# The second feed-forward of an attention, expert and feed-forward kernel: from one pass over its inner dimension to two

## The chip, the cores and the metric

The kernel runs on one core of one Trainium2 chip. The core has a matrix engine (PE, with PEld for the loading of its stationary operands), a vector engine (DVE), an activation engine (ACT), a general engine (POOL) and a queue engine that only issues transfers (SP). ACT and POOL can issue transfers too, each from its own row of instructions. The metric is the device time of one execution in microseconds (us), lower is better; the time to beat is the median of three runs.

## The reference, cut to what matters

```python
def reference(**kwargs):
    attn_out = _attn_ref(q, k, v)          # local + downsampled attention, 4 x 8 heads, 576 tokens, 64 each
    x = attn_out.transpose(0, 2, 1, 3).reshape(2304, 512)
    x = _moe_ref(x, w_gate, w1, w2)        # 8 experts, 288 tokens each
    return _moe2_ref(x, w_in, w_out)       # the second feed-forward

def _moe_ref(x, w_gate, w1, w2):
    ...                                    # greedy: the largest logits first, at most 288 tokens per expert
    for e in range(E):
        mask = assigned == e
        h = np.maximum(x[mask] @ w1[e], 0.0)      # 512 -> 1024
        out[mask] = h @ w2[e]                     # 1024 -> 512

def _moe2_ref(x, w_in, w_out):
    h = x @ w_in                                  # 512 -> 2048
    sp = np.where(h > 20.0, h, np.log1p(np.exp(np.minimum(h, 20.0))))
    g = h * np.tanh(sp)
    return (g @ w_out).astype(np.float32)         # 2048 -> 512
```

The host hands `w_in` and `w_out` over as 64-bit floats.

## The kernel before

**The number format.** Matrix products are made to near float32 precision out of a faster format: each operand is split into a high part (a cast, L623 on ACT or L621 on DVE, tiles `wah`, `wbh`, `gh`) and a low part (operand minus high part, L626 on POOL or DVE, tiles `wal`, `wbl`, `gl`), and each product is three matmuls (`mm3`, L631 to L633). Only the first expert, E0, is "plain" (`N32 = 1`): it multiplies unsplit float32 (L707).

**The stages.** The front end (attention, tokens 0 to 2303) writes `x` to DRAM. Then come eight routing phases, each of which finds the 288 tokens of one expert by many small DVE and PE steps, and eight experts E0 to E7. Expert k gathers its rows of `x` (L650, transfers issued by POOL) and computes; its result, split into high and low parts, goes to a ring of 768 tokens in on-chip memory, `Yh` and `Yl`. The second feed-forward runs in groups: M4 takes four tiles of 128 tokens out of the ring, M2 two. There are five groups, four M4 and one M2 at the end, called M#0 to M#4 here. `ORDER` puts experts and groups in a row: R0, N2, R1, E0, E1, M4, E2, E3, M4, E4, E5, M4, E6, E7, M4, M2; the two numbers behind a name are how many routing steps and how many pieces of narrowing (below) are put beside each of its steps. The instructions of each engine then follow a scheduler's order, and each engine runs its own row in order.

**Narrowing.** `Narrow` turns the 64-bit words of `w_in` and `w_out` into float32, in 32 pieces of 128x512. A piece is loaded by SP (L541, tile `n`) or sits in its final place already, passes ACT (L565, L567), DVE (L570, L573, L575, L578), POOL or DVE (L581, L583), and ends with an addition on POOL (L585) that puts the float32 weights into `wM_sb`, where they stay.

**A step of a group.** An M4 group has 16 steps, one for each slice f of 128 of the 2048 inner columns; the M2 group has 8 steps of two slices. In each step the weights of the slice are split anew (`split`: `wah`/`wal` of `w_in`, `wbh`/`wbl` of `w_out`), since the parts are not kept; PE makes `hm` (12 matmuls of 512 columns, of 256 where the tokens wrap around the ring and in M#4); ACT and DVE turn it into the activation, by turns: ACT L782, DVE L783, ACT L784, L785, L786, DVE L791, L792, L794, ACT L797 (`gh`), DVE L798 (`gl`); and PE adds `g` times `w_out` into `oa` some steps later (12 matmuls of 512 columns for four tiles). After the last slice the result is doubled into `osb` (L755 ACT, L757 DVE) and POOL scatters it to the output (L758).

**The buffers.** The raw words of the expert weights, `wraw` (L711, loaded by SP in pieces of 128x1024 4-byte words), and the raw pieces `n` of narrowing share a ring of three slots (`NRW`).

Of the kernel before, what the change touches and what calls it, by code (L numbers as in the profile page):

```python
# [57 lines left out]
class Attn:  # L58
# [190 lines left out]
    def emit(self, nar=None, rload=None):  # L249
# [65 lines left out]
class Router:  # L315
# [47 lines left out]
    def phase(self, k):  # L363
# [111 lines left out]
        V.tensor_scalar_add(ig, it, 1152.0)  # L475
        ip = self.psr.tile([96, 3], F32, name="ip", tag="rt")
# [18 lines left out]
        self.out[k] = idx, exi  # L495
# [3 lines left out]
POOLN = 4  # L499
NV = 3  # L500
N32 = 1
PE4 = 2
COPY2, COPY4 = 4, 8
LASTM = 1
LIGHT, PN1, GL1, T1 = 0, 1000, 1, 0
LAG2 = 3
NMI, NRW, NWA, NWB, NGS = 4, 3, 3, 6, 4
# [11 lines left out]
class Narrow:  # L519

    def __init__(self, nc, a, ne, zp):
        self.nc, self.a, self.zp = nc, a, zp
        self.ne = ne
        self.raw = {}
        self.n = 0

    def load(self, i, n=1, eng=None):

        s = (i if i < self.ne else i - self.ne) + 1
        t = self.a['wM_t'][s >= self.ne]
        s0 = s - self.ne * (s >= self.ne)
        (eng or self.nc.sync).dma_start(t[:, s0:s0 + n].rearrange("p s n -> p (s n)").bitcast(I32), self.a['wM'].rearrange("p f n -> p (f n)")[:, 512 * i:512 * (i + n)].bitcast(I32))
        for j in range(n):
            self.raw[i + j] = t[:, s0 + j].bitcast(I32).rearrange("p (n t) -> p n t", t=2)

    def stage(self, i):
        st = self.raw[i] = self.st.tile([128, 512, 2], I32, name="n64", tag="wraw")
        f, h = divmod(i, 2)  # L540
        self.nc.sync.dma_start(st.rearrange("p n t -> p (n t)"), self.a['wM'][:, f, 512 * h:512 * h + 512].bitcast(I32))  # L541

    def slot(self, f, s):
        return self.a['wM_t'][f >= self.ne][:, f - self.ne * (f >= self.ne), s]
# [5 lines left out]
    def steps(self):  # L550
# [5 lines left out]
        f, h = divmod(i, 2)  # L556
        b = {}
        def begin():
            if i not in self.raw:
                self.stage(i)  # L560
            st = self.raw.pop(i)
            z = self.zp.tile([128, 512], F32, name="nz")
            b.update(z=z, zi=z.bitcast(I32), w=self.slot(f, slice(512 * h, 512 * h + 512)), hi=st[:, :, 1], lo=st[:, :, 0])
            b['u'] = b['w'].bitcast(I32)
            nc.scalar.activation(out=b['z'], in_=b['hi'].bitcast(F32), func=AF.Abs)  # L565
            if i % NV:
                nc.scalar.activation(out=b['lo'].bitcast(F32), in_=b['lo'].bitcast(U32), func=AF.Copy, scale=2.0 ** -52)  # L567
# [16 lines left out]
        def end():  # L584
            nc.gpsimd.tensor_tensor(out=b['w'], in0=b['w'], in1=b['z'], op=ALU.add)  # L585
        return [begin, clip, bits, sign, power, low, end]

class FFN:

    LAG = 2  # L590

    def __init__(self, nc, tc, ctx, a, ps, slot):
        self.slot = slot
        self.nc, self.tc, self.a, self.ps = nc, tc, a, ps
        P = lambda n, b: ctx.enter_context(tc.tile_pool(name=n, bufs=b))
# [18 lines left out]
    def split(self, src, pool, nm):  # L614
# [4 lines left out]
        self.ncopy += 1  # L619
        if self.ncopy % self.copyn == 0:  # L620
            nc.vector.tensor_copy(wh, src)  # L621
        else:
            nc.scalar.copy(wh, src)  # L623
# [20 lines left out]
    def gather(self, k, idx):  # L644
        nc = self.nc
        nc.sync.dma_start(self.a['ilist'][288 * k:288 * k + 288, :].rearrange("(g p) o -> p (g o)", g=3), idx)
        rows = []
        for g in range(3):
# [3 lines left out]
            rows.append(xr)  # L652
        return rows

    def expert(self, k, rows, exi):
# [20 lines left out]
        def second(j, w2, hh, hl):  # L676
# [9 lines left out]
            if j == 7:  # L686
# [3 lines left out]
                for c in range(4):  # L690
                    for s0, s1 in pieces:
# [3 lines left out]
                                                in1=self.Yh[:, c, q:q + s1 - s0].bitcast(F32), op=ALU.subtract)  # L695
        for j in range(8):
# [26 lines left out]
    def group(self, t0, nt, last=False):  # L723

        nc, ps = self.nc, self.ps
        n = 128 * nt

        ms = [512 // n] * (16 * n // 512)
        if last and n < 512:
            ms[len(ms) - LASTM:] = [1] * (512 // n * LASTM)  # L730
        q = 128 * t0 % RING
        cols = [(0, n)] if q + n <= RING else [(0, RING - q), (RING - q, n - RING + q)]
        ixs = self.ix.tile([128, 4], I32, name="ixs")
        nc.sync.dma_start(ixs[:, 0:nt], self.a['ilist'][128 * t0:128 * (t0 + nt), :].rearrange("(t p) o -> p (t o)", p=128))
# [111 lines left out]
def body(nc, tc, a):  # L846
    with ExitStack() as ctx:
# [33 lines left out]
        for st in ORDER:  # L881
# [9 lines left out]
            if st[0] == 'E':  # L891
                while k not in rows:
                    bg[0]()
# [23 lines left out]
```

## Time and profile before

| | |
|---|---|
| median of three runs | 1049.76 us (1044.21 to 1050.76) |
| the profiled execution | 1053.49 us |
| its span, first to last instruction | 1051.7 us |
| mean granted PE clock | 0.929 |
| busy share: PE, PEld | 86%, 70% |
| busy share: DVE, ACT, POOL | 74%, 52%, 43% |
| read from and written to DRAM | 75.08 MB, 9.45 MB |

All the rows below are of the profiled execution, on its own scale of time. "Busy" is the time in which an engine executes; the matmuls of PE overlap at their ends, so the time from one start to the next tells the price of one. A row `A <- B` names the tile written and the tiles read.

### The profile page before, as it was taken

What the parts mean: (1) busy time and instruction counts of PE and PEld (TensorE: products, weight loads), DVE (VectorE), ACT (ScalarE), POOL (GpSimd) and SP (SyncE); (2) the same over time, 40 slices, a digit from 0 to 9 for tenths busy, and PEclk for the clock granted to TensorE, in tenths of its full rate; (3) what the DMA queues carried; (4) which work ended last, traced back from release to release, by engine and by line L of the source; (5) the groups of instructions that cost most, each with busy time, mean ns of one, the idle gap of its engine ahead of it and who ended that gap; (6) DMA issues with size and microseconds to landing.
All of it is one profiled execution on the core that took longest, in us unless ns stands there. A gap on an engine that the chain in (4) does not pass through costs nothing. (4 is left out here: it accounts for less than half of the span.)

```text
span 1051.7 us, 18198 instructions
## 1 busy us (share of the span) xinstructions
PE 903.4 (86%) x6676; PEld 739.2 (70%) x6676; DVE 780.6 (74%) x1798; ACT 545.7 (52%) x1310; POOL 448.1 (43%) x402
## 2 busy tenths in 40 slices
PE   5999994248778787998898999999899999999986
PEld 3777773135557565777897888898776798776774
DVE  4798988938958999878458767646877653777785
ACT  3677783103224455554436556555566555666663
POOL 4443403434636755326343322535432444333562
PEclk9999995558989898999899989999999999999998
DMA  8559516262253311015520001532200350000010
GB/s 210 150 158 274 177 55 230 80 163 81 63 124 101 80 41 60 1 44 162 125 78 1 1 1 41 165 120 62 22 1 21 131 173 1 1 1 1 1 41 20
DMA packets 32905, 85.69 MB, mean 81 GB/s; under 512 B 8912, under 2 KB 9168, under 8 KB 32048
## 3 DMA queue, kind: packets, MB, share of 16 engines
q1 hardware_dynamic: 26816, 67.23, 22.3%
q0 software_dynamic: 2976, 9.44, 4.0%
q10 hardware_dynamic: 3024, 7.87, 2.1%
q8 instruction: 52, 0.85, 0.3%
q14 instruction: 37, 0.30, 0.1%
HBM read 75.08 MB, written 9.45 MB: 80 GB/s over the span
## 5 line engine op out<-in xcount | busy, mean ns | idle before, releaser
L626 POOL TENSOR_TENSOR wal<-wM_sb,wah 128x512 fp32r<-128x512 f32 x80 | 115.1, 1441 | 164.2 <-ACT wah L623 160.0
L631 PE MATMUL hm<-Yh,wah 128*128 128x512 f32 (+1 forms) x384 | 135.6, 353 | 6.1 <-DVE eu L794 3.0
L633 PE MATMUL hm<-Yh,wal 128*128 128x512 f32 (+1 forms) x384 | 134.1, 349 | 2.6 <-POOL wal L626 2.6
L632 PE MATMUL hm<-Yl,wah 128*128 128x512 f32 (+1 forms) x384 | 133.6, 348 | 1.1 <-DVE Yl L694 1.1
L631 PE MATMUL oa<-wbh,gh 128*128 128x512 f32 x288 | 119.6, 415 | 11.4 <-ACT gh L797 11.0
L626 POOL TENSOR_TENSOR wal<-wraw,wah 128x512 fp32r<-128x512 f32 x56 | 73.9, 1325 | 119.9 <-ACT wah L623 119.4
L633 PE MATMUL oa<-wbh,gl 128*128 128x512 f32 x288 | 116.9, 409 | 3.1 <-DVE gl L798 3.1
L632 PE MATMUL oa<-wbl,gh 128*128 128x512 f32 x288 | 116.2, 403 | 0.0
L797 ACT CAST gh<-eu 128x512 fp32r<-128x512 f32 (+1 forms) x73 | 44.6, 611 | 105.8 <-DVE eu L794 105.8
L791 DVE SCALAR_TENSOR_TENSOR eu<-eu,r 128x512 f32<-128x512 f32 (+1 forms) x73 | 67.3, 922 | 39.0 <-ACT r L786 39.0
L631 PEld LDWEIGHTS hm<-Yh,wah 128*128 128x128 f32 x384 | 74.9, 195 | 17.1 <-ACT wah L623 4.7
L626 POOL TENSOR_TENSOR wbl<-wM_sb,wbh 128x512 fp32r<-128x512 f32 x40 | 53.8, 1345 | 75.0 <-ACT wbh L623 74.9
L633 PEld LDWEIGHTS hm<-Yh,wal 128*128 128x128 f32 x384 | 75.1, 196 | 11.1 <-POOL wal L626 3.2
L632 PEld LDWEIGHTS hm<-Yl,wah 128*128 128x128 f32 x384 | 74.9, 195 | 10.8 <-issue 1.6
L792 DVE SCALAR_TENSOR_TENSOR eu<-eu,r 128x512 f32<-128x512 f32 (+1 forms) x73 | 80.0, 1096 | 1.3
L784 ACT ACTIVATE eu<-eu,one_sb 128x512 f32<-128x512 f32 (+1 forms) x73 | 52.2, 716 | 48.2 <-DVE eu L783 47.5
L631 PEld LDWEIGHTS oa<-wbh,gh 128*128 128x128 f32 x288 | 56.7, 197 | 28.3 <-ACT gh L797 17.9
L633 PEld LDWEIGHTS oa<-wbh,gl 128*128 128x128 f32 x288 | 56.0, 195 | 23.6 <-DVE gl L798 12.0
L623 ACT CAST wah<-wM_sb 128x512 fp32r<-128x512 f32 x80 | 48.6, 612 | 45.6 <-PE hm L632 31.7
L631 PE MATMUL hp<-xh,wah 128*128 128x288 f32 x224 | 69.0, 309 | 0.2 <-DVE eu L794 0.2
L626 DVE TENSOR_TENSOR wbl<-wraw,wbh 128x512 fp32r<-128x512 f32 x56 | 41.6, 744 | 36.6 <-ACT wbh L623 32.2
L632 PE MATMUL ya<-gl,wbh 128*128 128x288 f32 x224 | 67.6, 302 | 0.0
(177 smaller groups left out, 2499.0 us busy)
## 6 DMA issues: line engine op xcount, KB each, us to landing
wraw<-in_wE_dram SPq DMA_DIRECT2D x56, 512.0 KB
n<-in_wM_dram SPq DMA_DIRECT2D x20, 512.0 KB
vw<-in_vw_dram SPq DMA_DIRECT2D x16, 315.0 KB
kT<-in_kT_dram SPq DMA_DIRECT2D x16, 291.0 KB
qT<-in_qT_dram SPq DMA_DIRECT2D x16, 288.0 KB
vd<-in_vd_dram SPq DMA_DIRECT2D x16, 288.0 KB
x_dram<-xr ACTq DMA_DIRECT2D x18, 256.0 KB
w<-in_wE_dram SPq DMA_DIRECT2D x16, 256.0 KB
```

Of the source, the lines that this page charges most:

```text
L623: nc.scalar.copy(wh, src)
L626: eng.tensor_tensor(out=wl, in0=src, in1=wh.bitcast(F32), op=ALU.subtract)
L631: mm(out, lh, rh, start=first, stop=False)
L632: mm(out, lh, rl, start=False, stop=False)
L633: mm(out, ll, rh, start=False, stop=last)
L784: nc.scalar.activation(out=u, in_=e, func=AF.Square, bias=one)
L791: nc.vector.scalar_tensor_tensor(out=u, in0=u, scalar=1.0, in1=r, op0=ALU.add, op1=ALU.mult)
L792: nc.vector.scalar_tensor_tensor(out=u, in0=u, scalar=2.0, in1=r, op0=ALU.subtract, op1=ALU.mult)
L797: nc.scalar.copy(gh[:, 0:w], e)
```

## The change

The groups take two tiles (256 tokens) and half of the inner dimension. Nine groups G (half 0) each write their sum, doubled, to a DRAM buffer `part`; nine groups P (half 1) load it, add it, and scatter the result. A group has four steps of two slices. So that the second pass can have the tokens again, each expert also writes its split result to a DRAM buffer `y_dram` (ACT issues the stores), and each P group loads its 256 tokens of it back into the ring (POOL issues the loads).

The split parts of the feed-forward's weights are made once, at the end of each piece of narrowing, and kept: the pieces of half 0 in `wM1`, on chip; those of half 1 (pieces 16 to 31) in the slot of the raw ring in which they were loaded, from where POOL stores them to the DRAM buffer `wB`. After E7 the pools of the experts are closed and eight transfers of 1 MB (POOL) fetch half 1 into `wM3`, in their place. The groups split no weights.

Besides: E1 is plain too (`N32 = 2`); the raw ring has four slots; no piece is loaded or narrowed during the front end; routing and narrowing have other rates; the list of tokens is written in rows; `eu`, `r` and `osb` have rings of their own.

```diff
-NRAW, NNAR, NKL, NSL, NKP, NSP = 6, 0, 24, 0.5, 42, 1.4
-N32 = 1
+N32 = 2
-NMI, NRW, NWA, NWB, NGS = 4, 3, 3, 6, 4
+NRW, NWA, NWB, NGS = 4, 3, 5, 4
+HC = 8
+LAGE, LAGM = 2, 3
 class Narrow:
...
+    def fetch(self, i, n, eng):
+        f = i // 2
+        t, f0 = self.a['wM_t'][-1]
+        eng.dma_start(t[:, f - f0:f - f0 + n // 2].rearrange("p f h n -> p (f h n)"), self.a['wB'][:, 1024 * (i - 2 * HC):1024 * (i - 2 * HC + n)])
...
         def begin():
-            if i not in self.raw:
-                self.stage(i)
-            st = self.raw.pop(i)
+            rt = self.st.tile([128, 1024], I32, name="n64", tag="wraw")
+            nc.sync.dma_start(rt, self.a['wM'].rearrange("p f n -> p (f n)")[:, 512 * i:512 * i + 512].bitcast(I32))
+            raw = rt.rearrange("p (n t) -> p n t", t=2)
+            st = self.place(i) if i < 2 * HC else rt.bitcast(F32R)
...
         def end():
-            nc.gpsimd.tensor_tensor(out=b['w'], in0=b['w'], in1=b['z'], op=ALU.add)
+            nc.gpsimd.tensor_tensor(out=b['t'], in0=b['t'], in1=b['z'], op=ALU.add)
+            h, l = b['st'][:, 0:512], b['st'][:, 512:1024]
+            nc.scalar.copy(h, b['t'])
+            nc.gpsimd.tensor_tensor(out=l, in0=b['t'], in1=h.bitcast(F32), op=ALU.subtract)
+            if i >= 2 * HC:
+                nc.gpsimd.dma_start(self.a['wB'][:, 1024 * (i - 2 * HC):1024 * (i - 2 * HC + 1)].bitcast(F32), b['st'].bitcast(F32))
...
+                for s0, s1 in pieces:
+                    q = (pos + s0) % RING
+                    for v, y in enumerate((self.Yh, self.Yl)):
+                        nc.scalar.dma_start(self.a['y_dram'][:, v, :, 288 * k + s0:288 * k + s1].bitcast(F32), y[:, :, q:q + s1 - s0].bitcast(F32))
...
-    def group(self, t0, nt, last=False):
+    def group(self, t0, half):
...
+        nt, n, m = 2, 256, 2
+        ms = [m] * (HC // m)
...
+        if half:
+            for v, t in enumerate((self.Yh, self.Yl)):
+                nc.gpsimd.dma_start(t[:, :, y], self.a['y_dram'][:, v, :, 128 * t0:128 * t0 + n])
...
+            for t in range(nt):
+                os[t] = self.mi.tile([128, 512], F32, name="osb")
+                nc.sync.dma_start(os[t], self.a['part'][128 * (t0 + t):128 * (t0 + t) + 128, :])
...
+                    if not half:
+                        o = self.mi.tile([128, 512], F32, name="osb")
                         nc.scalar.activation(out=o, in_=acc[t], func=AF.Copy, scale=2.0)
+                        nc.scalar.dma_start(self.a['part'][128 * (t0 + t):128 * (t0 + t) + 128, :], o)
+                        continue
+                    o = os[t]
+                    nc.vector.scalar_tensor_tensor(out=o, in0=acc[t], scalar=2.0, in1=o, op0=ALU.mult, op1=ALU.add)
...
             for i in range(m):
-                w1 = self.split(self.slot(f + i, slice(0, 512)), self.wa, "wa")
-                w2.append(self.split(self.slot(f + i, slice(512, 1024)), self.wb, "wb"))
...
+                w1 = self.slot(HC * half + f + i, 0)
...
-ORDER = 'R0 N2 R1 E0/0.6/2 E1/0.8/0.5 M4/1/1 E2/0.6/2 E3/0.8/0 M4/0.5/0 E4/0.3/0 E5/0/0 M4/0.9/0 E6/1.2/0 E7/0.3/0 M4/0.6/0 M2/0/0'.split()
+ORDER = ('R0 R1 E0/0/1 R2 E1/0/1 G/1 E2/0.8/0.3 G/0.8 E3/0.85/0.3 G/0.8 E4/0.85/0.3 G/0.8 E5/0.85/0.3 G/0.8 E6/0.85/0.3 G/0.8 E7/0/0.6 N'
+         + ' G' * 3 + ' P' * 9).split()
...
             if st[0] == 'N':
-                advance(1, k)
+                while nar.n < 32:
+                    nar.piece()
+                f.flush()
+                ctx_e.close()
+                wM.append((P("wM3", ctx).tile([128, 16 - HC, 2, 1024], F32R, name="wM3_sb"), HC))
+                for i in range(2 * HC, 32, 2):
+                    nar.fetch(i, 2, nc.gpsimd)
                 continue
```

ACT in the middle of the last four-tile group of before, M#3, where `eu` and `r` are the activation's tiles and `wbh`, `wah` the high parts of the weights:

```order
L784 ACTIVATE eu<-eu,one_sb 128x512
L785 ACTIVATE r<-eu,one_sb 128x512
L623 CAST wbh<-wM_sb 128x512
L786 ACTIVATE r<-r 128x512
L623 CAST wah<-wM_sb 128x512
L782 ACTIVATE eu<-hm 128x512
L797 CAST gh<-eu 128x512
L784 ACTIVATE eu<-eu,one_sb 128x512
L785 ACTIVATE r<-eu,one_sb 128x512
L786 ACTIVATE r<-r 128x512
L623 CAST wah<-wM_sb 128x512
L782 ACTIVATE eu<-hm 128x512
```

ACT in the middle of the groups P after the change:

```order
L776 ACTIVATE eu<-eu,one_sb 128x512
L777 ACTIVATE r<-eu,one_sb 128x512
L778 ACTIVATE r<-r 128x512
L785 CAST gh<-eu 128x512
L774 ACTIVATE eu<-hm 128x512
L776 ACTIVATE eu<-eu,one_sb 128x512
L777 ACTIVATE r<-eu,one_sb 128x512
L778 ACTIVATE r<-r 128x512
L785 CAST gh<-eu 128x512
L774 ACTIVATE eu<-hm 128x512
```

The two casts of a step (L623) are gone; the five instructions of the activation stand alone, and each step now follows on the one before.

POOL in the last groups of before, where L758 is the scatter of the output:

```order
L758 DMA out_dram<-osb,ixs 2304x512 x2
L626 TENSOR_TENSOR wal<-wM_sb,wah 128x512 x2
L758 DMA out_dram<-osb,ixs 2304x512 x2
L626 TENSOR_TENSOR wbl<-wM_sb,wbh 128x512
L626 TENSOR_TENSOR wal<-wM_sb,wah 128x512 x2
L626 TENSOR_TENSOR wbl<-wM_sb,wbh 128x512
L626 TENSOR_TENSOR wal<-wM_sb,wah 128x512 x2
L626 TENSOR_TENSOR wbl<-wM_sb,wbh 128x512
```

POOL after the last expert in the changed kernel, where `wM_sb` is half 1 of the weights' parts and L754 the scatter:

```order
L615 TENSOR_TENSOR wal<-wraw,wah 128x512 x2
L528 DMA wM_sb<-wB 128x2048 x8
L726 DMA Yh<-y_dram 128x4x256
L726 DMA Yl<-y_dram 128x4x256 x2
L726 DMA Yh<-y_dram 128x4x256
L726 DMA Yl<-y_dram 128x4x256
L726 DMA Yh<-y_dram 128x4x256
L726 DMA Yl<-y_dram 128x4x256
L726 DMA Yh<-y_dram 128x4x256
L754 DMA out_dram<-osb,ixs 2304x512 x2
L726 DMA Yl<-y_dram 128x4x256
```

Subtractions between the scatters have given way to transfers alone: eight fetches of weights, then the loads of the split tokens for four groups ahead of the first scatter.

SP at the loads of the last expert before, where `wraw` is the raw words of its weights:

```order
L734 DMA ixs<-ilist 128x2x1
L711 ISA
L711 DMA wraw<-in_wE_dram 128x1024
L711 ISA
L711 DMA wraw<-in_wE_dram 128x1024
```

SP at the loads of the last expert after, where `n_...` are raw pieces of narrowing, in the same ring of slots:

```order
L547 DMA n_9399<-in_wM_dram 128x1024
L702 ISA
L702 DMA wraw<-in_wE_dram 128x1024
L702 ISA
L702 DMA wraw<-in_wE_dram 128x1024
L547 DMA n_9496<-in_wM_dram 128x1024
L702 ISA
L702 DMA wraw<-in_wE_dram 128x1024
L547 DMA n_9550<-in_wM_dram 128x1024
L702 ISA
```

Four pieces of narrowing now stand between the loads of this expert (three of them in these rows); in each of E2 to E6 there are two or three.

## Rows read from the trace of the kernel before

**Rows 1.** Busy time by stretch; columns: stretch, its length, PE, PEld, DVE, ACT, POOL, clock.

```profile
225.70:304.20 78.50, 58.96 (x349) 38.73 (x349) 55.73 (x138) 18.25 (x38) 36.91 (x29) 0.80 0.38 103
304.20:346.30 42.10, 37.13 (x334) 32.78 (x334) 36.11 (x98) 17.46 (x35) 25.39 (x21) 0.96 0.34 101
346.30:477.90 131.60, 115.74 (x685) 85.65 (x684) 120.34 (x248) 71.40 (x122) 59.82 (x42) 0.94 0.18 45
477.90:553.70 75.80, 70.17 (x606) 65.02 (x605) 45.99 (x136) 29.73 (x67) 38.00 (x34) 0.95 0.43 121
553.70:665.30 111.60, 101.76 (x717) 89.25 (x716) 84.09 (x162) 66.38 (x113) 31.73 (x27) 0.97 0.05 15
722.20:829.50 107.30, 97.10 (x463) 72.63 (x461) 85.14 (x141) 64.94 (x116) 37.73 (x36) 0.98 0.17 36
829.50:884.40 54.90, 54.90 (x408) 54.18 (x409) 24.92 (x46) 29.33 (x63) 31.25 (x26) 1.00 0.39 127
884.40:979.20 94.80, 88.02 (x362) 67.27 (x361) 67.59 (x86) 59.18 (x103) 31.43 (x23) 0.98 0.00 1
979.20:1044.80 65.60, 57.57 (x313) 48.50 (x311) 52.69 (x71) 39.12 (x72) 32.79 (x25) 0.92 0.04 17
```

**Rows 2.** Timeline of PE: 512 columns; columns: start, duration, instruction.

```profile
756.65 0.39 PE L633 MATMUL oa<-wbh,gl 128*128 128x512 f32 x1
...
757.78 0.39 PE L632 MATMUL oa<-wbl,gh 128*128 128x512 f32 x1
```

**Rows 3.** Timeline of PE: 256 columns.

```profile
1004.34 0.28 PE L631 MATMUL hm<-Yh,wah 128*128 128x256 f32 x1
...
1004.93 0.28 PE L633 MATMUL hm<-Yh,wal 128*128 128x256 f32 x1
```

**Rows 4.** Timeline of PE in E0, 288 columns, plain float32; a row may hold several.

```profile
237.06 0.75 PE L707 MATMUL hp<-xh,w 128*128 128x288 f32 x2
...
238.65 1.24 PE L707 MATMUL hp<-xh,w 128*128 128x288 f32 x4
```

**Rows 5.** Timeline of PE in E5, 288 columns, split operands.

```profile
697.10 0.29 PE L633 MATMUL hp<-xh,wal 128*128 128x288 f32 x1
...
697.90 0.29 PE L633 MATMUL hp<-xh,wal 128*128 128x288 f32 x1
```

**Rows 6.** Timeline of DVE in M#3.

```profile
909.20 0.69 DVE L792 SCALAR_TENSOR_TENSOR eu<-eu,r 128x512 f32<-128x512 f32 x1
...
915.32 1.67 DVE L792 SCALAR_TENSOR_TENSOR eu<-eu,r 128x512 f32<-128x512 f32 x1
```

**Rows 7.** Timeline of POOL in M#3.

```profile
914.87 1.56 POOL L626 TENSOR_TENSOR wal<-wM_sb,wah 128x512 fp32r<-128x512 f32 x1
```

**Rows 8.** Waits of PE in M#3 and M#4; columns: total, times, longest.

```profile
PE oa L631 <- ACT gh L797: 5.8, 6, 2.0
PE hm L631 <- DVE eu L794: 3.0, 2, 2.4
```

**Rows 9.** The page, costliest groups: the first, the splits of `w_in`.

```profile
L626 POOL TENSOR_TENSOR wal<-wM_sb,wah 128x512 fp32r<-128x512 f32 x80 | 115.1, 1441 | 164.2 <-ACT wah L623 160.0
```

**Rows 10.** Groups of narrowing by line; columns: shortest, median, longest, first and last start.

```profile
L570 DVE TENSOR_SCALAR nz<-nz x32: 406/414/1516, 152.2 to 407.4; 128x512 f32<-128x512 f32 x32
...
L585 POOL TENSOR_TENSOR wM_sb<-wM_sb,nz x32: 1262/1344/2246, 157.0 to 416.2; 128x512 f32<-128x512 f32 x32
```

**Rows 11.** Timeline of SP: the load of a piece.

```profile
389.07 0.33 SPq L541 DMA_DIRECT2D n<-in_wM_dram  x1
```

**Rows 12.** Timeline of POOL: the end of the same piece.

```profile
405.14 1.66 POOL L585 TENSOR_TENSOR wM_sb<-wM_sb,nz 128x512 f32<-128x512 f32 x1 [0.96 <-DVE nz L583]
```

**Rows 13.** Groups by line: the gathers that POOL issues.

```profile
L650 POOL DMA_INDIRECT xrow<-x_dram,idx x24: 923/1104/3337, 214.2 to 832.2; - x24
```

**Rows 14.** The page, queues: packets, MB, share of 16 engines' span.

```profile
q1 hardware_dynamic: 26816, 67.23, 22.3%
q0 software_dynamic: 2976, 9.44, 4.0%
```

More of the change, by code (lines that the diff above doesn't have):

```diff
@@ L519, with __init__, place, slot @@
 class Narrow:
-    def __init__(self, nc, a, ne, zp):
+    def __init__(self, nc, a, zp):
         self.nc, self.a, self.zp = nc, a, zp
-        self.ne = ne
-        self.raw = {}
         self.n = 0
[L529 to L539, printed above, removed]
-        f, h = divmod(i, 2)
-        self.nc.sync.dma_start(st.rearrange("p n t -> p (n t)"), self.a['wM'][:, f, 512 * h:512 * h + 512].bitcast(I32))
-    def slot(self, f, s):
-        return self.a['wM_t'][f >= self.ne][:, f - self.ne * (f >= self.ne), s]
+    def place(self, i):
+        f, h = divmod(i, 2)
+        t, f0 = next(x for x in self.a['wM_t'] if x[1] <= f < x[1] + x[0].shape[1])
+        return t[:, f - f0, h]
+    def fetch(self, i, n, eng):
+        f = i // 2
+        t, f0 = self.a['wM_t'][-1]
+        eng.dma_start(t[:, f - f0:f - f0 + n // 2].rearrange("p f h n -> p (f h n)"), self.a['wB'][:, 1024 * (i - 2 * HC):1024 * (i - 2 * HC + n)])
+    def slot(self, f, h):
+        t = self.place(2 * f + h)
+        return t[:, 0:512], t[:, 512:1024]
     def piece(self):
@@ L786, in group @@
             nc.scalar.activation(out=r, in_=r, func=AF.Exp, scale=-1.0)
-            if light and T1:
-                nc.scalar.activation(out=u, in_=u, func=AF.Identity, bias=one)
-                nc.gpsimd.tensor_tensor(out=u, in0=u, in1=r, op=ALU.mult)
-            else:
-                nc.vector.scalar_tensor_tensor(out=u, in0=u, scalar=1.0, in1=r, op0=ALU.add, op1=ALU.mult)
+            nc.vector.scalar_tensor_tensor(out=u, in0=u, scalar=1.0, in1=r, op0=ALU.add, op1=ALU.mult)
             nc.vector.scalar_tensor_tensor(out=u, in0=u, scalar=2.0, in1=r, op0=ALU.subtract, op1=ALU.mult)
@@ L869, in routing @@
                     yield
-                rows[k] = f.gather(k, r.out[k][0])
+                rows[k] = f.gather(k, r.out[k][0], r.out[k][2])
                 yield
@@ L874, in body @@
         bg = routing().__next__, nar.piece
-        t0, m, n = 0, [0, 0], [0, 0]
+        t0, m, n = [0, 0], [0, 0], [0, 0]
         def advance(c, x):
@@ L882, in body @@
             st, *rate = st.split('/')
[L883 removed]
             if st[0] == 'N':
[L885 removed]
+                while nar.n < 32:
[5 more added lines that the diff above has]
+                    nar.fetch(i, 2, nc.gpsimd)
                 continue
[L887 removed]
+            if st[0] in 'RE':
+                k = int(st[1:])
                 while k not in rows:
                     bg[0]()
[L890 to L893 removed]
+                if st[0] == 'R':
+                    continue
                 steps = f.expert(k, rows[k], r.out[k][1])
             else:
[L896 to L897 removed]
+                h = 'GP'.index(st[0])
+                steps = f.group(t0[h], h)
+                t0[h] += 2
             for _ in steps:
```

129 lines of the change are left out of this document (48 added, 81 removed).

## The prediction

> **What bounds the kernel now.** I read the busy times by stretch first. The five groups of the second feed-forward take 131.6, 111.6, 107.3, 94.8 and 65.6 us [rows 1], together 510.9 of the span of 1051.7 us. Next comes what PE needs for them. A matmul of 512 columns starts 0.226 us after the one before (five steps in 1.13 us) [rows 2], one of 256 columns 0.118 to 0.12 us [rows 3]. M#0, M#2 and M#3 have 384 matmuls of 512 columns, 87.0 us; M#1, whose tokens wrap around the ring, has half of its `hm` in two pieces, 384 x 0.119 + 192 x 0.2265 = 89.2; M#4 has 192 x 0.119 + 96 x 0.2265 = 44.6. The sum is 394.8, so 116.1 us of these stretches is excess: 44.6, 22.4, 20.3, 7.8 and 21.0.
>
> Where does the excess come from? M#3 has neither routing nor narrowing beside it, and only 7.8 us. Its waits say what is late: `oa` waits for ACT's `gh`, `hm` for DVE's `eu` [rows 8], so the activation's chain through ACT and DVE, not PE. That chain is slow where POOL subtracts: the same DVE instruction takes 0.69 us and, beside a subtraction of POOL, 1.67 [rows 6, 7]. In M#4 DVE is busy 52.69 of 65.6 us, 6.6 per step of two slices, where PE needs 5.6 [rows 1]: it is bound by DVE, with splits in it. The rest of the excess is routing: M#1 lies 111.6 - 89.2 - 7.8 = 14.6 above M#3's manner with about one phase beside it, so a phase costs some 14 us of PE's path, and M#2 gives 12.5. I put 14 in M#0, which makes 41 for the five groups. And M#0 holds 131.6 - 87.0 - 7.8 - 14 = 22.8 us for seven pieces of narrowing, 3.3 us each, with DVE at 120.34 of 131.6 us [rows 1]. The experts E6 and E7 show the other end: 54.9 us, all of it PE, DVE 24.92 [rows 1].
>
> **The change part by part.**
>
> *Matmuls of the groups.* All groups now have two tiles. `hm` is 1728 matmuls of 256 columns, `oa` is 864 of 512: 205.6 + 195.7 = 401.3, against 394.8: **+6.5 us**.
>
> *Excess of the groups.* The change takes 80 splits of two weights out of the groups: 120 subtractions on POOL (1.44 us each for the 80 of `w_in` [rows 9]), 40 on DVE, and 160 casts. A step of two slices then has PE at 12 x 2 x 0.119 + 12 x 0.2265 = 5.6 us; DVE and ACT did at most 4.2 and 3.7 us in M#3's steps with the splits still in them (67.59 and 59.18 over 16) [rows 1]. So PE becomes the bound. I keep the routing's 41 us, since the same phases stand beside the middle groups and experts. Of the other 75 us I keep: in the six groups G between the experts, with POOL at work on routing and on the next expert's splits, M#3's 7.8/16 = 0.49 us for each of 24 steps, 12; in the twelve groups after E7, where POOL only issues transfers, 0.05 for each of 48 steps, 2.4; one start behind E7 and one end of the last group, for which I take half of M#4's 21, 10. That is 24.4, so **-50.6 us**. Between the ends: were M#3's 0.49 to hold in all 72 steps, it would be 21 us less gain.
>
> *Narrowing, moved and made dearer.* Each piece gains a copy on ACT and a subtraction on POOL; the nearest prices are 1.34 us for the addition L585 [rows 10] and 1.44 for a split [rows 9]. Pieces 16 to 31 now lie beside E2 to E7, two or three in each and four in E7. Nothing in the trace shows narrowing beside split experts. The bounds are 0 (the experts leave DVE over half idle, 24.92 of 54.9) and 3.3 us each as in M#0, where DVE was full; the experts' row is the nearer one, but the pieces also take slots of the raw ring (first rival), so I take 1.3: **+21 us**, of 0 to 53.
>
> *The start.* Some four pieces leave the front end and nine in all leave the time before M#0. A piece costs DVE three instructions of 0.41 us [rows 10] and sometimes a fourth, 1.5 us. In R1 and E0 DVE has 55.73 of 78.5 us and PE, at a clock of 0.80, only 58.96 [rows 1]: the routing's DVE steps set the pace. I take -6 there (0 to -13.5 for nine pieces) and -3 in the front end (0 to -6). E1 becomes plain: 128 matmuls at 0.245 us (two more in 1.24 - 0.75) to 0.31 (1.24/4) [rows 4] make 31 to 40, against 192 at 0.80/6 = 0.133 [rows 5], 25.6. I take 35.5, 10 more on PE, but E1 now takes 42.1 us with PE at 37.13 [rows 1], and loses its splits and its narrowing: +5 (0 to 10). Together **-4 us**. The loads of E0's weights now stand behind ten loads of pieces in SP's row, and ACT stores x ahead of them as before; all of it is ready before R0 ends, so I cost it at nothing, with at most 18 us (one piece's way, below) if it is not.
>
> *New transfers.* Stores to `y_dram` and `part` are issued by ACT, which is off the path (29.33 of 54.9 us in E6 and E7). After E7 POOL issues eight fetches of 1 MB and the loads of tokens. Queue q1 moved 67.23 MB in 22.3% of the span, 287 GB/s, POOL's queue q0 9.44 MB in 4.0%, 224 GB/s [rows 14]: 8.4 MB take 29 to 37 us. They are hidden behind three groups G, 12 x 5.6 = 67 us; then 1 MB per P group of 22.4 us is 47 GB/s. The added waits on POOL (for the ring's tokens, for `osb`) have only transfers behind them. **0 us**; if the cover were gone, 37.
>
> The gathers that POOL issues take 1.10 us by their median and 3.34 at the longest [rows 13], while DVE was busy beside them. The Trainium skill, "SBUF — State Buffer", section "SBUF: two separate sides", warns that a transfer issued by POOL waits for its descriptors while DVE runs a two-port operation. It speaks against putting all loads of the second pass on POOL. By the row's excess of 2.2 us per transfer, eight fetches would be 18 us later, 55 instead of 37, still within the 67: the sum would be the same.
>
> *Sum.* 6.5 - 50.6 + 21 - 4 = -27: a span of 1024.6 us. The profiled execution was 1053.49, 1.8 above its span, so 1026.4; the median of the runs is 0.9965 of it, so **1022 us**.
>
> **The rivals.**
>
> *A, slower: the raw ring.* A piece of half 1 keeps its slot from its load until its parts are stored. The load of one piece was issued at 389.07 and its addition ended at 406.80 [rows 11, 12], 17.7 us; copy, subtraction and store add about 0.6 + 1.3 + 1.8 (0.5 MB at 287 GB/s), 21.4 in all. An expert asks for a weight piece every 54.9/16 = 3.4 us, and four slots come round in 14. The slot is some 7 us late; where that falls on half of the 16 pieces, eight stalls of 7 us are 56 in place of my 21, and with the loads behind them in SP's row late as well, 1022 + 35 + some 5 = 1062. For it: one ring, in order, and E7 with four pieces among eight weights. Against it: SP runs ahead during each group G, 22 us in which no expert weight is asked for. It decides from 3.7 us per piece.
>
> *B, the second pass is fed late.* If POOL's queue moves less than 8.4 MB in 67 us, 125 GB/s, the groups P wait; at 90 GB/s 93 us, 26 late: 1048, no change. Against it: both queues' rates.
>
> *C, the shape of M#4 stays.* Its steps look like those of after, and take 65.6/8 = 8.2 us where PE needs 5.6. If not the splits but the length of the activation's chain were the cause, with `eu` and `r` two deep, half of the 2.6 in 72 steps would be 94 us: about 1090. Against it: DVE's 6.6 us per step fall to at most 4.2.
>
> *D, narrowing is as dear as in M#0*, 3.3 us for each of 16 pieces: +32, 1054, no change.
>
> *E, more gain.* The pieces vanish in the experts' idle DVE (-21), or the phases get cheaper beside an unloaded DVE (12 for 14 us each, -8): 993 to 1008.
>
> **How the numbers follow.** The measurement tells about 1% from no change: below 1039.3 faster, above 1060.3 slower. My forecast, 1008 to 1039, has 0.60; E 0.12, also faster; B and D 0.15, within 1%; A 0.09 and C 0.04, slower. So faster 0.72, same 0.15, slower 0.13. The range goes from 990 (E's lower end) to 1055 (D), and leaves out A, C and a little below.
>
> **What would show it.** The groups P should run at 22 to 23 us each with PE near 100% and no POOL instruction but transfers; the time from the last matmul of E7 to the end should be near 285 us (12 x 22.4, a start, an end, the scatter). DVE's slow L792 should be gone there. The experts E2 to E7 should take 28 to 31 us each; over 34 speaks for A or D, and the waits of SP for stores, with PE or ACT waiting for `wraw`, tell A. P groups over 25 us mean B (PE waiting for transfers) or C (PE waiting for `gh`). E0 should begin no later than now. The prediction is wrong if the middle, from E2 to E7, grows by more than the groups give back.

## The result, and the profile after

The changed kernel takes 1021.05 us by the median of the runs on record, against 1048.91 before: a ratio of 0.9723, 95% interval 0.968 to 0.9767. Forecast were 1022 us and a range of 990 to 1055. One execution of the changed kernel, at 2084.69 us with matmuls of 256 columns at 0.54 us each instead of 0.28, counts in that median, but not in the ratio nor in what follows. The profile below is of another execution of the same code (run e0): span 1016.4, time 1018.18 us.

Busy time by stretch, after; columns as in [rows 1] (behind the clock stand the busy share of the DMA engines and GB/s), and the stretches in order: E0; E1 up to the first `hm` of a group; E2 with a group; E5 with a group; E6 with a group; E7; the three groups G behind it; the nine groups P.

```profile
225.20:294.40 69.20, 52.51 (x309) 33.99 (x307) 51.42 (x118) 15.50 (x30) 41.23 (x32) 0.85 0.35 108
294.40:336.40 42.00, 42.00 (x284) 28.70 (x282) 23.15 (x85) 8.89 (x19) 9.83 (x12) 0.96 0.42 143
364.70:435.80 71.10, 63.00 (x512) 56.38 (x511) 53.11 (x134) 30.87 (x65) 25.96 (x23) 0.95 0.36 122
575.00:645.90 70.90, 62.60 (x524) 56.51 (x523) 48.65 (x132) 31.78 (x65) 27.53 (x30) 0.95 0.41 130
645.90:709.40 63.50, 53.17 (x345) 50.24 (x345) 37.92 (x64) 33.52 (x65) 33.21 (x28) 0.89 0.53 177
709.40:738.80 29.40, 29.40 (x210) 28.68 (x209) 12.72 (x21) 11.69 (x25) 11.23 (x9) 1.00 0.29 91
738.80:806.00 67.20, 66.62 (x448) 61.51 (x447) 39.72 (x66) 43.00 (x70) 8.75 (x14) 1.00 0.67 213
806.00:1010.50 204.50, 201.78 (x1285) 181.26 (x1283) 121.99 (x200) 113.29 (x183) 27.48 (x28) 0.99 0.27 75
```

The last two rows answer to M#3 and M#4 of [rows 1]: 271.7 us with PE at 268.4 of them, POOL's share only the issuing of transfers, DVE at 60%. A group P takes 22.0 us (`hm` starts at 865.1 and again at 887.1), and its matmuls stand as close as in [rows 2, 3]:

```profile
864.92 0.39 PE L622 MATMUL oa<-wM_sb,gl 128*128 128x512 f32 x1
865.15 0.28 PE L620 MATMUL hm<-Yh,wM_sb 128*128 128x256 f32 x1
865.27 0.28 PE L621 MATMUL hm<-Yl,wM_sb 128*128 128x256 f32 x1
```

PE's waits from the end of E7 to the end (total, times, longest), where [rows 8] had 8.8 us in these two kinds alone:

```profile
PE hm L620 <- DVE eu L782: 1.7, 2, 1.2
PE oa L620 <- ACT gh L785: 1.5, 1, 1.5
```

And the activation's DVE instructions in the groups P (shortest, median, longest), L780 being the former L792 that took 0.69 or 1.67 us [rows 6]:

```profile
L780 DVE SCALAR_TENSOR_TENSOR eu<-eu,r x37: 424/692/694, 805.9 to 1007.2; 128x512 f32<-128x512 f32 x35, 128x256 f32<-128x256 f32 x2
...
L775 DVE TENSOR_SCALAR eu<-eu x36: 283/419/783, 808.7 to 1004.7; 128x512 f32<-128x512 f32 x34, 128x256 f32<-128x256 f32 x2
```

So the end of the program is as forecast. The middle is not: the experts with routing and narrowing beside them take 69 to 71 us with their group, where a group is 22.3 us of PE and an expert 27.4 [rows 1], E6 63.5 though no routing is left, and PE stands idle for 10 us of these at a lower clock (0.89).

Where the pieces run in time is not where they stand in the program. By POOL's additions (L574) in this trace, two, three, two and two of the pieces 16 to 31 end in the cycles of E2 to E5, five in E6's and one in E7's (the first of the sixteen ends before E2): three of the four that stand among E7's loads are loaded and narrowed while PE is still at E6 and its group. A cycle is here an expert with its group, as in the rows above.

A balance of the two profiles, in us of excess over PE's own need, an expert counted with 27.45 us: from the first `hm` of a group to the end of E7, before 538.1 - 427.9 = 110.2, after 402.4 - 298.5 = 103.9; behind E7, before 160.4 - 131.6 = 28.8, after 271.7 - 267.5 = 4.2. That is -31. The matmuls add 6.5, and the first `hm` comes at 336.4 instead of 346.3: -10. Together -34.5, against spans 35.3 apart.

### The profile page after: what moved, and what is told of

The parts are those of the page before. It is cut to its first block, busy times and chain, and to the rows that moved or that the text cites. A ratio compares the mean times of both kernels' runs of the same rounds, so it can differ in the third digit from the quotient of the medians.

```text
span 2082.9 us, 19063 instructions
## 1 busy us (share of the span) xinstructions
PE 2024.5 (97%) x7188; PEld 1586.2 (76%) x7188; DVE 668.0 (32%) x1733; ACT 501.0 (24%) x1197; POOL 325.2 (16%) x348
## 4 chain that ended last, share of the span: by engine, by line
PE 62%; issue 20%; POOL 2%; DVE 1%; DMA 0%; POOLq 0%; ACT 0%; DVEq 0%
PE hm L621 5%; PE hm L620 5%; PE hm L622 5%; PE oa L621 5%; PE oa L622 5%; PE oa L620 4%; PE hp L698 4%; PE ya L670 4%; PE hp L620 3%; PE cnt L411 3%; PE hp L621 3%; PE ya L621 3%; PE hp L622 3%; PE ya L620 3%; PE ya L622 3%
## 5 line engine op out<-in xcount | busy, mean ns | idle before, releaser
L620 PE MATMUL hm<-Yh,wM_sb 128*128 128x256 f32 x576 | 305.5, 530 | 0.0
L622 PE MATMUL hm<-Yh,wM_sb 128*128 128x256 f32 x576 | 305.4, 530 | 0.0
L621 PE MATMUL hm<-Yl,wM_sb 128*128 128x256 f32 x576 | 304.9, 529 | 0.0
L620 PEld LDWEIGHTS hm<-Yh,wM_sb 128*128 128x128 f32 x576 | 243.0, 422 | 13.9 <-issue 13.2
L621 PEld LDWEIGHTS hm<-Yl,wM_sb 128*128 128x128 f32 x576 | 242.3, 421 | 11.4 <-issue 11.4
L622 PEld LDWEIGHTS hm<-Yh,wM_sb 128*128 128x128 f32 x576 | 246.1, 427 | 0.1
L621 PE MATMUL oa<-wM_sb,gh 128*128 128x512 f32 x288 | 240.3, 835 | 0.0
L620 PE MATMUL oa<-wM_sb,gh 128*128 128x512 f32 x288 | 238.5, 828 | 0.4 <-ACT gh L785 0.4
L622 PE MATMUL oa<-wM_sb,gl 128*128 128x512 f32 x288 | 238.1, 828 | 0.0
L775 DVE TENSOR_SCALAR eu<-eu 128x512 f32<-128x512 f32 (+1 forms) x73 | 33.2, 454 | 423.3 <-ACT eu L774 423.3
L622 PEld LDWEIGHTS oa<-wM_sb,gl 128*128 128x128 f32 x288 | 101.0, 351 | 61.3 <-issue 60.1
L620 PEld LDWEIGHTS oa<-wM_sb,gh 128*128 128x128 f32 x288 | 104.9, 364 | 54.0 <-issue 52.6
L621 PEld LDWEIGHTS oa<-wM_sb,gh 128*128 128x128 f32 x288 | 106.2, 369 | 52.2 <-issue 51.8
L620 PE MATMUL ya<-gh,wbh 128*128 128x288 f32 x192 | 108.8, 567 | 0.0
L621 PE MATMUL hp<-xl,wah 128*128 128x288 f32 x192 | 108.5, 565 | 0.0
L622 PE MATMUL hp<-xh,wal 128*128 128x288 f32 x192 | 107.6, 560 | 0.0
```

The costliest lines, as they stand in the source:

```text
L620: mm(out, lh, rh, start=first, stop=False)
L621: mm(out, lh, rl, start=False, stop=False)
L622: mm(out, ll, rh, start=False, stop=last)
L775: nc.vector.tensor_scalar_min(e, e, EXP20)
```

## The experiments

Each kernel was timed beside the kernel before on the same chip. Ratios are to the kernel before, with 95% intervals; differences between two kernels are taken between their ratios, 0.001 being 1.05 us. By the intervals such a difference is uncertain by some 5 to 10 us.

**e0, the changed kernel again.** No edit.

> The changed kernel again, for a profile at the usual clock. The theory (splits leave the groups, so PE paces them): groups P at 22 to 23 us each, the time from the end of E7 to the end near 285 us, experts E2 to E7 at 28 to 31 us. Rival (a smaller gain in the groups, and more of it at the start): groups over 24 us, and E0 begins over 10 us earlier.

Measured 1018.27 us, ratio 0.9721 (0.9657 to 0.9784). Groups P 22.0 us and 277.6 us from E7's end to the end of the span (1016.4 - 738.8): the theory holds for the groups, the rival falls. E2 to E6 take more than the 28 to 31 us given; I come to that below.

**e1, the kernel before with one split per group.**

```diff
-                w1 = self.split(self.slot(f + i, slice(0, 512)), self.wa, "wa")
-                w2.append(self.split(self.slot(f + i, slice(512, 1024)), self.wb, "wb"))
+                if f + i == 0:
+                    one1 = self.split(self.slot(0, slice(0, 512)), self.wa, "wa")
+                    one2 = self.split(self.slot(0, slice(512, 1024)), self.wb, "wb")
+                w1 = one1
+                w2.append(one2)
```

> The kernel before, whose groups split only the first slice's weights and use these parts for all slices (152 of the 160 splits of the groups are left out, and the sums are of other weights). If the splits are what slows the groups, they give back most of the 75 us that are neither routing nor matmuls, less the narrowing of M#0: 40 to 50 us, about 1003 us, with M#3 near 88 and M#4 near 50 us. If the length of the activation's chain is the cause: 10 us or less, about 1040, M#4 still over 60 us.

Measured 989.41 us, ratio 0.9469 (0.9415 to 0.9523): 56 us less. M#0 to M#4 in it (columns as above):

```profile
340.40:463.60 123.20, 110.82 (x683) 82.81 (x681) 98.62 (x229) 61.56 (x101) 27.95 (x23) 0.94 0.20 51
535.90:633.00 97.10, 97.03 (x713) 86.07 (x713) 62.85 (x151) 53.70 (x87) 4.64 (x6) 1.00 0.03 7
690.70:789.30 98.60, 92.51 (x462) 73.24 (x461) 61.80 (x133) 57.30 (x96) 11.36 (x17) 0.98 0.18 39
844.20:926.50 82.30, 82.02 (x362) 67.35 (x361) 48.03 (x79) 49.27 (x79) 0.00 (x0) 1.00 0.00 1
926.50:977.10 50.60, 50.60 (x313) 45.35 (x312) 30.02 (x52) 29.57 (x51) 4.12 (x4) 1.00 0.06 22
```

Against [rows 1] the five groups lose 8.4, 14.5, 8.7, 12.5 and 15.0 us. M#3 and M#4 together take 132.9 where PE needs 131.6. The splits were the cause, and the activation's chain, whose length did not change, was not (rival C falls). M#0 keeps 36 us of excess, with seven pieces of narrowing and a routing phase.

**e2, the changed kernel with E1 split.**

```diff
-N32 = 2
+N32 = 1
```

> The changed kernel with E1 split as before, all else kept. My price of the plain E1 was +5 us (0 to 10), so 5 us less than the changed kernel, 1016. If the splits of E1 would stand beside routing that needs the same DVE and POOL, as the rival has it, there is no gain or a loss of up to 8 us.

Measured 1008.28 us, ratio 0.965 (0.9594 to 0.9706): 7.5 us less by the ratios, 10 by the medians. In its trace the first `hm` of a group starts at 320.0, not 336.4. Of these 16 us, 6 lie ahead of E0's first matmul (219.0 against 225.2), which comes anywhere from 218.8 to 228.0 in the runs with a plain E1. From there to the first `hm` it is 101.0 us against 111.1, and the other runs bear this out: 99.7 and 103.7 us with E1 split (e11, e12), 110.6 to 111.9 with a plain E1 (e3 to e10). So the plain E1 costs 7 to 12 us there, not 5.

**e3, the changed kernel without pieces 16 to 31.**

```diff
-        if i == 32:
+        if i == 16:
...
-                while nar.n < 32:
+                while nar.n < 16:
...
-        eng.dma_start(t[:, f - f0:f - f0 + n // 2]...., self.a['wB'][...])
+        eng.dma_start(t[:, f - f0], self.a['wE'][0:2, f - f0].rearrange("h p n -> p h n").bitcast(F32R))
```

> The changed kernel without the narrowing of pieces 16 to 31 (half 1 of the weights is left out: no loads of raw pieces, no stores, and the eight fetches read expert weights in its place, at the same size). My price of these pieces was 21 us (0 to 53), 1.3 each: 1000 us. If they vanish in the experts' idle engines: 1018 to 1021. If they hold the raw ring as rival A has it: under 985, with experts E2 to E7 shorter by over 5 us each.

Measured 980.79 us, ratio 0.9362 (0.9288 to 0.9437): 37.7 us less, 2.4 for each piece, not 1.3. The rows that answer to E2, E5, E6 and E7 above:

```profile
364.50:430.30 65.80, 63.23 (x517) 56.66 (x515) 42.80 (x124) 28.31 (x59) 18.02 (x16) 0.97 0.30 100
559.00:626.20 67.20, 62.79 (x533) 56.38 (x532) 41.23 (x120) 28.22 (x58) 17.54 (x21) 0.97 0.32 98
626.20:673.50 47.30, 47.30 (x341) 45.30 (x341) 23.52 (x44) 28.11 (x55) 14.04 (x11) 1.00 0.43 138
673.50:703.90 30.40, 30.40 (x215) 29.52 (x214) 9.80 (x19) 11.05 (x23) 6.44 (x5) 1.00 0.10 36
```

E6 with its group falls from 63.5 to 47.3 us, all of it PE; the cycles of E2 to E5, which have routing, by 5.3, 5.6, 4.9 and 3.7; E7 not at all. By where the pieces run that is 2.2 us for each of the nine in E2 to E5 and 3.2 for each of the five in E6. And a routing phase costs the middle some 14 us (367.1 - 298.5 = 69 in all, five phases), as forecast: the pieces were the term that I priced too low. Which of their costs? ACT's waits from 351 us, early in the first group, to the end of E7 (total, times, longest), with the pieces and then without:

```profile
ACT n L576 <- POOL nt L574: 31.2, 11, 4.7
ACT wah L612 <- DMA wraw<-in_wE_dram: 19.6, 8, 3.7
...
ACT n L576 <- DVE G L405: 9.3, 2, 5.2
```

```profile
ACT wah L612 <- DMA wraw<-in_wE_dram: 16.9, 6, 4.1
```

SP's waits for stores of pieces, with them:

```profile
SPq L702 <- DMA wB<-n: 47.8, 7, 13.7
...
SPq L547 <- DMA wB<-n: 31.9, 4, 20.8
```

SP does wait for the stores, 80 us in 11 places, as rival A has it; but ACT's waits for `wraw` hardly grow (19.6 against 16.9). New are 40 us in which ACT stands in its row at the cast that ends a piece. All of these waits end with POOL's addition: also the two that the view puts down to DVE, whose casts begin 0.03 us after L574 has ended, as the others do. The chain of waits in E6 shows both kinds of links in a row (start, duration, what):

```profile
654.91 4.95 DMA wB<-n
...
660.00 3.65 DMA n<-in_wM_dram
...
663.67 0.68 ACT nz L553
...
664.38 0.47 ACT wbh L612
664.85 0.53 ACT wah L612
...
665.45 1.70 POOL wal L615
...
669.21 1.66 POOL nt L574
...
670.89 0.02 ACT n L576
...
671.42 0.61 ACT wah L612
...
672.34 0.52 ACT wbh L612
...
672.88 1.82 DVE wbl L615
...
674.80 4.23 DMA wraw<-in_wE_dram
...
679.12 0.63 ACT wah L612
```

A store, the next piece's load into the freed slot, ACT, the expert's casts, POOL's split, the addition of a piece, ACT's cast, the expert's next cast, a DVE split that lasts 1.82 us, and then a load of weights.

**e4, the slot free sooner** (rival A by itself).

```diff
+            st = self.place(i) if i < 2 * HC else None
...
+            h, l = (b['st'][:, 0:512], b['st'][:, 512:1024]) if i < 2 * HC else (b['z'].bitcast(F32R), b['t'].bitcast(F32R))
...
+                o = 1024 * (i - 2 * HC)
+                nc.gpsimd.dma_start(self.a['wB'][:, o:o + 512].bitcast(F32), b['z'])
+                nc.gpsimd.dma_start(self.a['wB'][:, o + 512:o + 1024].bitcast(F32), b['t'])
```

> The changed kernel, in which the parts of pieces 16 to 31 are made in the piece's two work tiles and stored from there in two halves, so that the raw ring's slot comes free after the last read of the raw words instead of after the store. Leaving these pieces out gave back about 37 us, 2.3 each. If that is the ring's slots held by pieces (rival A), half or more of it goes: under 1002 us. If it is work of DVE, ACT and POOL or the order on them, the time stays within 6 us of the changed kernel's 1018 to 1021 (two more transfers per piece on POOL speak for a little more).

Measured 1015.69 us, ratio 0.970 (0.9674 to 0.9726): 2 us. SP's waits for stores are gone, but others have taken their place, for the last reader of the piece's raw words (L569, and L571 with another 14.8 us in 3 places):

```profile
SPq L704 <- POOL nz L569: 34.0, 5, 17.4
...
SPq L547 <- POOL nz L569: 19.1, 3, 12.1
```

In e0 a piece holds its slot for 15 to 30 us, and some 8 of them lie behind that last read. These 8 us, about what rival A counted as late, are worth 2. ACT's waits for `wraw`, 16.1 us here, are no longer than in e3 without the pieces (16.9). So rival A falls as it was put; whether it would help to shorten the time before the last read was not tried.

**e5, the cast on POOL.**

```diff
-            nc.scalar.copy(h, b['t'])
+            nc.gpsimd.tensor_copy(h, b['t'])
```

> The changed kernel with the cast at the end of a piece on POOL instead of ACT, so that ACT no longer stands in its row until POOL's addition is done (40 us of such waits in 13 places between E1 and the end of E7) with the experts' casts behind it. If that blocking is the price of the pieces: 15 us or more less than the changed kernel, under 1005. If the price is DVE's work, or POOL's load that slows DVE: no change, or up to 10 us more for 32 casts of 1.3 us on POOL.

Measured 1019.77 us, ratio 0.9731 (0.9703 to 0.9759): no change. That does not clear ACT's waits: the edit gives POOL 32 casts more, and e9 below shows that POOL's steps are dear, so a gain on ACT may be hidden by a loss on POOL.

**e6, pieces without their DVE steps.**

```diff
-        return [begin, clip, bits, sign, power, low, end]
+        return [begin, low, end] if i >= 2 * HC else [begin, clip, bits, sign, power, low, end]
```

> The changed kernel, in which pieces 16 to 31 keep their loads, ACT and POOL steps and stores, but the four or five DVE steps of each are left out (a third of them get a POOL and an ACT step in place of a DVE one; the fetches read expert weights of the same size, so half 1 of the weights is not the reference's). If DVE's work is the price, some 2 us in each piece on an engine that the routing's phases wait for: 20 us or more of the 37 come back, under 1000 us. If it is the ring or ACT's blocking: less than 10 us come back, over 1008.

The fetches read expert weights as in e3, and the five pieces whose product DVE makes have it on POOL here, with a scaling on ACT, so that the gain is rather too small. Measured 1011.0 us, ratio 0.9634 (0.9604 to 0.9664): 9 us of the 37. DVE is a part, not the whole.

**e7, e4 and e5 together.** Both edits above.

> The two edits of the runs before at once: the slot of the raw ring free sooner, and the cast on POOL. Alone they gave 2 us back and none of the 37 that the pieces cost. If these were two links of one chain of waits, each hiding the other, both together give 10 us or more, under 1009. If the price is the work itself on DVE and POOL: 1013 to 1021, as each alone.

Measured 1012.38 us, ratio 0.9649 (0.9597 to 0.9701): 7.6 us less than e0 by the ratios, 6 by the medians, with an interval of 5 to either side of its own ratio. It lies between the two expectations; whether the two links hide each other is not shown.

**e9, pieces without their POOL steps.**

```diff
         def low():
+            if i >= 2 * HC:
+                return
...
+            if i < 2 * HC:
                 nc.gpsimd.tensor_tensor(out=b['t'], in0=b['t'], in1=b['z'], op=ALU.add)
...
+            if i < 2 * HC:
                 nc.gpsimd.tensor_tensor(out=l, in0=b['t'], in1=h.bitcast(F32), op=ALU.subtract)
```

> The changed kernel, in which pieces 16 to 31 keep their loads, ACT and DVE steps and stores, but the two or three POOL computations of each are left out (the fetches read expert weights of the same size, so half 1 of the weights is not the reference's). Without their DVE steps 9 us of the 37 came back. If POOL is the larger part (some 4 us of POOL in each piece, ahead of the experts' low parts and beside DVE's routing): 15 us or more come back, under 1005. If no single engine is the price but the length of the chain through the ring: less than 10, over 1009.

A third of the pieces loses a DVE step here as well, the product. Measured 996.64 us, ratio 0.950 (0.9471 to 0.953): 23 us of the 37. POOL's steps are the larger part, with all that waits on them: without them ACT's cast no longer waits for an addition, and the slot comes free sooner. Which of these it is, POOL's busy time or the waits behind it, e9 does not separate. The gains of e9, e6 and e7 overlap, so they do not add up to the whole.

**e10, half 1 narrowed late.**

```diff
+EARLY = 28
+SEQ = list(range(16)) + list(range(EARLY, 32)) + list(range(16, EARLY))
...
+            st = self.place(i) if i < EARLY else rt.bitcast(F32R)
...
+                nar.st = ctx_n.enter_context(tc.tile_pool(name="n_raw", bufs=3))
...
+ORDER = ('R0 R1 E0/0/1 R2 E1/0/1 G/1 E2/0.8/0.125 G/0.8 E3/0.85/0.125 G/0.8 E4/0.85/0.125 G/0.8 E5/0.85/0.125 G/0.8 E6/0.85 G/0.8 E7 N'
+         + ' G/0/1' * 3 + ' F' + ' P' * 9).split()
```

> A changed place: pieces 28 to 31 stay beside E2 to E5 and go through DRAM as now, pieces 16 to 27 are narrowed beside the three groups G behind E7, straight into their final place, where POOL is idle and PE has 67 us of its own work. If the pieces cost what they displace (2.3 us beside the experts, where routing and the splits need the same engines, and little where PE is ahead): 25 us or more less than the changed kernel, 985 to 997. If a piece costs some 2 us wherever it stands, as the first stage and M#0 suggest: 1013 to 1021.

Measured 1038.16 us, ratio 0.9864 (0.9811 to 0.9917): 15 us more by the ratios, a miss of my expectation, and worse than its rival's. The three G groups and the first three P groups:

```profile
725.20:750.40 25.20, 16.93 (x111) 16.23 (x110) 21.67 (x33) 15.60 (x30) 10.98 (x9) 0.80 0.40 125
750.40:778.90 28.50, 24.30 (x145) 21.67 (x144) 28.19 (x36) 15.20 (x27) 16.69 (x13) 0.94 0.38 101
778.90:811.90 33.00, 24.96 (x145) 21.44 (x143) 30.73 (x39) 18.91 (x33) 19.83 (x15) 0.95 0.32 89
811.90:835.90 24.00, 23.96 (x144) 21.97 (x145) 15.03 (x22) 15.02 (x25) 6.25 (x8) 0.93 0.61 181
835.90:862.80 26.90, 23.38 (x145) 20.90 (x144) 15.72 (x25) 14.25 (x23) 3.54 (x4) 0.95 0.20 54
862.80:885.20 22.40, 22.40 (x145) 20.44 (x144) 13.62 (x23) 13.50 (x23) 3.37 (x5) 0.98 0.42 118
```

In e0 the same three groups, cut in the same way at the first `hm` of each, are:

```profile
738.80:753.90 15.10, 14.52 (x110) 13.83 (x109) 8.27 (x16) 10.18 (x18) 5.78 (x10) 1.00 0.94 334
753.90:776.40 22.50, 22.50 (x146) 20.53 (x145) 14.38 (x24) 15.07 (x25) 1.48 (x2) 1.00 0.83 276
776.40:798.90 22.50, 22.50 (x146) 20.54 (x145) 12.56 (x21) 13.53 (x23) 1.48 (x2) 1.00 0.32 83
```

With four pieces each they take 25.2, 28.5 and 33.0 us instead of 15.1, 22.5 and 22.5, and the first three groups P behind them 7 us more than in e0. DVE is busy for nearly all of two groups G, and PE's clock is at 0.80 in the first. The clip of the activation, 0.42 us by its median above, has here (shortest, median, longest):

```profile
L779 DVE TENSOR_SCALAR eu<-eu x8: 414/1303/1887, 748.4 to 811.8; 128x512 f32<-128x512 f32 x8
```

And PE waits for the activation's last DVE step in the three groups (total, times, longest), where e0 has 0.6 us:

```profile
PE hm L624 <- DVE eu L786: 20.5, 6, 8.3
```

So an idle POOL and a busy PE do not hide a piece: the activation's DVE steps are late by it. From E7's end to the last matmul it is 305.5 us, 34 more than in e0, 2.8 for each of twelve pieces. In E6's cycle, which has no piece here, the 16 us came back (47.3 us, as in e3). But the single piece that stays beside each of E2 to E5 left these cycles at 69 to 71.5 us, 3.8 to 5.8 more than in e3 and as long as with two or three pieces: there the first piece costs nearly all. In three of the four ACT stands for 5.1 or 5.2 us at the piece's cast until POOL's addition is done, with the expert's casts behind it; that this is the reason was not tried.

**e11, the same with E1 split.** Both edits.

> As the run before, with E1 split as in the kernel before. The plain E1 cost 8 to 10 us in the changed kernel: so 8 to 10 us less than the run before, 976 to 989.

Measured 1029.6 us, ratio 0.9813 (0.9784 to 0.9842): 5 us less than e10 by the ratios, 9 by the medians. Its absolute number missed with e10's.

**e12, the pieces' arithmetic on DVE, with e4 and E1 split.**

```diff
+            if i % NV and i < 2 * HC:
...
+            eng = nc.gpsimd if i < 2 * HC else V
+            eng.tensor_tensor(out=b['t'], in0=b['t'], in1=b['z'], op=ALU.add)
...
+            eng.tensor_tensor(out=l, in0=b['t'], in1=h.bitcast(F32), op=ALU.subtract)
```

The condition on `i % NV` stands in two places: ACT's scaling and POOL's product are kept for half 0 alone, and DVE makes the product of half 1.

> The changed kernel with E1 split again (8 to 10 us less by itself, 1008 measured), the raw ring's slot free sooner (2 less), and the POOL arithmetic of pieces 16 to 31 (product, addition, subtraction, some 4 us a piece) on DVE, some 2 us a piece. Without the POOL steps 22 us of the pieces' 37 came back, without the DVE steps 9. If POOL's 4 us are the price, by what waits for POOL and by the DVE instructions they slow: 990 to 1000. If any engine's time is as dear on DVE, which the routing waits for: 1003 to 1012.

Measured 991.41 us, ratio 0.9495 (0.9457 to 0.9534): 5% faster than the kernel before and 24 us less than the changed kernel, with the reference's whole computation. Against e2 it is 16 us, of which e4's share is some 2. So here POOL's steps are dearer than the same arithmetic on DVE, though DVE is the fuller engine. The edit also spares ACT the scaling of eleven pieces, and ACT's cast waits for DVE's addition instead of POOL's; how much of the gain is due to these is not separated.

## Why the prediction was right, and where it was not

**Splits out of the groups: right, and larger.** I took -50.6 us of excess. e1 shows the cause (56 us for the splits alone), and behind E7 4.2 us of excess are left, where I had kept 2.4 for the steps and 10 for a start and an end. What the step is worth with narrowing out of the middle is read from e3: 367.1 - 298.5 = 69 us of excess up to E7's end and 4 behind it, against 139 before, 66 less; this and my 50.6 both hold the pieces that left M#0. The splits had also slowed what stood beside them: in e1 the three groups with routing lose 31.6 us together, where M#3's manner, 7.8 each, gives 23.4.

**Narrowing, moved and made dearer: the mis-sized term.** I took 1.3 us a piece, 21 in all, of 0 to 53; it measured 37.7, 2.4 a piece, about midway between 1.3 and rival D's 3.3; in E6's cycle, where five pieces run, it is 3.2. The step that failed was to hold the experts' row the nearer one because DVE is over half idle there. e9 and e6 show POOL's steps, with what waits on them, to be the larger part and DVE's the smaller: the figure to read was POOL's 31.25 of 54.9 us in E6 and E7 [rows 1], on which a piece lays some 4 us beside the experts' low parts. Rival A's mechanism is in SP's waits, but the stores' part of it is worth 2 us by itself, and ACT's waits for `wraw` did not grow. E7's row above, all PE, is no test of it: only one of E7's four pieces is loaded while PE is at E7.

**The start: -4 forecast; the sum was near, its parts were not.** The kernel to compare with is e1, whose front end is that of before; the profiled execution of before was late by itself, with E0's first matmul at 231.3 against 226.0. The first `hm` comes at 340.4 in e1 and at 336.4 in e0: 4 us. The plain E1 costs 7 to 12 us of that (e2), the upper end of my 0 to 10: the 10 us more on PE stand nearly whole, and the splits that E1 lost paid for little of it. From E0's first matmul to the first `hm` e1 takes 114.4 us and e2, also with E1 split, 101.0: 13 us, where I had put 6 for the pieces; routing stands there at other rates too, so the share of the pieces is not separated. The front end is open: R0 begins at 160.2 in e0 and at 163.9 in e1, but its tally comes at 202.0 and 201.5, and in the kernel before, which has the code of e1 up to there, R0 begins at 168.8: executions of one code differ by more.

**New transfers: right, at nothing.** POOL's issues behind E7 (start, duration, instruction, and in brackets the idle time before it), then the time to the landing of a fetch by its median, in us:

```profile
739.53 4.28 POOL L528 DMA_DIRECT2D wM_sb<-wB  x8 [9.16 <-PE ya L622]
...
773.98 0.74 POOL L726 DMA_DIRECT2D Yl<-y_dram  x1 [20.86 <-PE hm L622]
```

```profile
wM_sb<-wB POOLq DMA_DIRECT2D x8, 1024.0 KB, 16.5
```

Eight fetches were issued in 4.28 us and PE waited for none of their data (its waits behind E7 are the two lines above), with DVE at 39.72 of 67.2 us beside them. The rule of the Trainium skill, "SBUF — State Buffer", section "SBUF: two separate sides", that such a transfer waits for descriptors while DVE runs a two-port operation, took nothing from this kernel; what DVE's two-port operations alone would do is not shown by these runs. Rival B falls.

**What would show it.** The groups P, the 285 us behind E7 (277.6) and the clean L780 came about as written. "28 to 31 us" for each of E2 to E7 was wrong in itself: it left out the routing phases that I had kept in the sum, some 14 us for each of five. By it I would have read A or D from any outcome.

So the mechanism was right, but that 1022 came so near is luck in part: two errors went against each other, the excess falling by 66 instead of 51 and the pieces taking 38 instead of 21.

## What to carry to other kernels

Work that is taken out of a loop and done once is not free: here 66 us of excess went and 38 came back with the narrowing beside the experts. Price the moved work on every engine that it uses at the new place (here POOL's steps were the larger part), not only on the engine that you know as the bound. Look up in the trace where the moved work runs: an engine that is ahead runs it earlier than the program's order suggests. Where POOL and DVE can both do a step, try the fuller DVE: in e12, 2 us there cost less than 4 on POOL.

## What the runs showed of the hardware that was not expected

An instruction of DVE with one input, the activation's clip on 128x512, took 0.42 us by its median in the groups P of e0, where POOL only issues transfers (L775), and 1.30 us beside narrowing on POOL (L779 of e10); [rows 6] had shown the like for one with two inputs. The Trainium skill, "SBUF — State Buffer", section "Who interferes with whom", counts such an operation among those that can take the ports that DVE and POOL share; e10's row agrees.

The granted clock of PE was 0.89 in E6's cycle and 0.80 in the first group of e10, where PE had waited, against 1.00 in the same stretches of e3 and e0, where it had not. What part of the pieces' price is slower matmuls was not separated.
